# Fp32 value loads, bf16 bias factors and an earlier first FFN block in a one-core attention and maxout-FFN kernel

## The chip, the core and the metric

The kernel runs on one core of a Trainium2 chip. Its time is the device time of one execution in microseconds. Lower is better. The core's engines are named as in the profile: PE is TensorE (PEld its weight loads), ACT is ScalarE, DVE is VectorE, POOL is GpSimd and SP is SyncE. SP, ACT and POOL issue DMAs, and each does so in its own program order.

## What is computed

Attention with a relative position bias, and behind it a feed-forward layer that takes the largest of three products:

```python
batch, n_heads, seq, head_dim = (8, 8, 576, 64)          # 32 bias buckets
scores = (q @ k.T) / sqrt(64) + bias_table[bucket(|i - j|)]
attn = exp(scores - max); attn /= sum
x = (attn @ v)                                            # as [4608 tokens, 512]
h = max(x @ w1, x @ w2, x @ w3)                           # d_ff = 768
out = h @ w_out                                           # [4608, 512] float32
```

All inputs are float32 in DRAM. The bias of a head depends on |i - j| alone, and is the same for every distance beyond some 128.

## The kernel before

**The bias.** Instead of adding the bias to the scores, the kernel multiplies the exponentials by exp(bias - bias at the far end), which is 1 outside a band around the diagonal. The factors are made once: a one-hot matrix `pick` of distances by buckets and the `table` are multiplied on PE (`spread`, fp32), ACT takes the exponential with the negated far value `negc` as its bias into `w_sb` (and a mirrored half), ACT writes this row to DRAM (`w_dr`), and SP reads it back with shifted rows as `hank`, in two loads of four heads each. `times_band`, `times_band_pair` (DVE) multiply the exponentials by parts of `hank`; `bandt`, a turned copy that POOL makes in `make_bandt`, serves the left keys.

**Attention.** A batch is 8 heads in four pairs (`hp` 0 to 3). For a pair, keys and queries lie transposed in `kT` and `qT`. `scores` makes products of two key tiles with 256 queries for both heads in PSUM and one exponential of 128x1024 on ACT into `e4`. 576 is 4 x 128 + 64: the last 64 keys of both heads are handled by `left_keys`, the last 64 queries by `left_queries`, both into `el`. `attend(b, hp, e4, el, half)` makes the sums with the values (`vx`, tails in `vt`) for half 0 (256 queries) or half 1 (the other 320), and returns `quotients`, which divides on DVE into `x_sb`. `x_transposes` turn that into `xT`, FFN's input.

**Batch 0** ("batch one" of the title) has no time to prefetch, so it is written out by hand. Heads 0 to 3's first two query tiles and all keys come as fp32 by the SP and ACT queues into borrowed parts of `xT` (`q32`, `k32`), and are cast by `cast_keys`, `act_copy` and `dve_copy`; the other queries, the tails and all the values come through POOL's queue, which casts on the way (`load_main`, `load_tail`, and for `vx` one load for each head). Products on zeros (`on_zeros`, `keep_warm`) run on PE in idle stretches. The batch has two passes over the four pairs: pass one takes queries 0 to 255, pass two the rest. In pass one a step makes `visit` (two `scores`), the next pair's `first_transposes`, and left keys; the bands of pairs 0 and 1 are multiplied in its last step. The sums of a pair are put in the list `late` and popped by `next_late` in pass two: half 0 of pairs 0 and 1 in its first step, of pairs 2 and 3 in the second, then half 1 of pair 0 in the third. `behind` holds a step's band multiplies with `hank` and `bandt` (`late_bands`, `products`) for the next step.

**The queues.** `inorder` keeps an instruction in program order on its engine. On POOL the order is: batch 0's loads; `load_w(0)`; then `load_second`: keys and queries of batch 1's first pair, tails, `load_w(1)`, `make_bandt`, the other keys and queries, a spread of the first pair, batch 1's values and `load_w(2)`.

**FFN.** `add_ffn` cuts the work on a group of tokens into portions and puts them in `pending`; `fill(n)` takes portions of up to n products of a block and issues them between attention's. In a portion list f, m, g are the first, second and third gate's products of a block and o the output. For the first 256 tokens `add_ffn(0, QS)` is called in pass two's fourth step; their third gate and output are kept in `deferred` and come with the next group.

Of the kernel before, what the change touches and what calls it, by code (L numbers as in the profile page):

```python
# [39 lines left out]
def kernel(  # L40
# [12 lines left out]
    nc = tc.nc  # L53
# [180 lines left out]
    q32 = borrow(2, 2 * KT * D).rearrange("p (t h d) -> p t h d", t=2, h=KT)  # L234
# [25 lines left out]
    table = stage.tile([NB, H], F32, name="table")  # L260
    nc.gpsimd.dma_start(out=table[:], in_=bias_table)
    ident = const.tile([P, P], BF16, name="ident")
# [5 lines left out]
    nc.scalar.preload_act_table_set("natural_log_exp_and_others")  # L268
    for h in range(2):
        load_32(q, h, q32, nc.sync, 2)  # L270
    for h in range(2, H):
        load_32(k, h, k32, nc.sync)
# [6 lines left out]
    nc.gpsimd.iota(ids[:, 0:NW], pattern=[[1, NW]], base=0, channel_multiplier=0)  # L279
    nc.gpsimd.iota(ids[:, NW:], pattern=[[0, 1]], base=0, channel_multiplier=1)  # L280
    pick = xT[0:NB, 1, spare].bitcast(F32)
    zeros = xT[:, 1, NTOK - CH :]
    inorder(nc.vector.memset(zeros, 0.0))
    constants(0)
    inorder(nc.vector.memset(qtail[1][64:, :, :], 0.0))
    dve_copy(pick[:], ids[:])
    ranges = _bucket_ranges(S, NB, 128)
# [3 lines left out]
    for vv in range(single, NB):  # L291
        if ranges[vv] is not None:
            lo, hi = ranges[vv]
            assert hi <= P or vv == NB - 1
            inorder(nc.vector.memset(pick[:, lo : min(hi, NW)], float(vv)))
    inorder(nc.vector.tensor_scalar(
        out=pick[:, 0:NW], in0=pick[:, 0:NW], scalar1=pick[:, NW:], scalar2=None, op0=ALU.is_equal,
    ))
    constants(1)
    load_main(q, 0, KT, H, batch[0][0], 0, 2)  # L300
    load_tail(k, 0, 0, H, k_diag)
    load_main(q, 0, 0, H, batch[0][0], 2, KT)
    load_q_tail(0)
    load_tail(v, 0, 0, H, v_diag)
    for h in range(H):
        in_turn(0, nc.gpsimd.dma_start(out=vx[0][:, :, h, 0:D], in_=main_part(v, 0)[:, :, h, :]))
# [13 lines left out]
    on_zeros(warm[:, 0:CH], 9)  # L320

    act_copy(batch[0][0][:, 0:2, 0:2, :], q32[:, :, 0:2, :])
    w_sb = stage.tile([H, WL], BF16, name="w_sb")

    def spread_bias():
        spread = ps_a.tile([H, NW], F32, tag="a", name="spread")
        mm(spread[:], lhsT=table[:], rhs=pick[:, 0:NW])
        negc = stage.tile([H, 1], F32, name="negc")
        inorder(nc.vector.tensor_scalar(
            out=negc[:], in0=spread[:, HALF:], scalar1=-1.0, scalar2=None, op0=ALU.mult,  # L330
        ))
        for out_, in_ in ((w_sb[:, HALF:], spread[:]), (w_sb[:, 0:HALF], spread[:, HALF:0:-1])):
            inorder(nc.scalar.activation(out=out_, in_=in_, func=ACTF.Exp, bias=negc[:]))
        inorder(nc.scalar.dma_start(out=w_dr[:], in_=w_sb[:]))
# [58 lines left out]
    def ffn(t0, nt, last, tiled=False):  # L393
# [278 lines left out]
        else:  # L672
# [75 lines left out]
    def first_transposes(hp):  # L748
# [6 lines left out]
        for t in range(2):  # L755
            tr(tq[:, P * t : P * t + P], batch[0][0][:, t, hs, :].rearrange("p h d -> p (h d)"), ident[:])
        for t in range(KT):
            tr(tp[:, P * t : P * t + P], batch[0][1][:, t, hs, :].rearrange("p h d -> p (h d)"), ident[:])
        e = K if hp < 2 else L
        if e > K:  # L760
            tr(tp[:, K:L], ktail[0][:, hp, :], ident[:])
        dve_copy(qk[0][0][:, hp, 0:QS], tq[:, 0:QS])
        dve_copy(qk[0][1][:, hp, 0:e], tp[:, 0:e])
# [289 lines left out]
    cast_keys(0)  # L1053
    spread_bias()
    first_transposes(0)
    on_zeros(warm[:, 0:CH])
    for h0 in (0, KT):
# [10 lines left out]
    load_w(0)  # L1068
    batch[1] = load_tiles()
# [30 lines left out]
    for hp in range(HP):  # L1100
# [12 lines left out]
        if hp == HP - 1:  # L1113
            bands(0)
            bands(1)
        late.append(lambda hp=hp, e4=e4, el=el: attend(0, hp, e4, el, 0))
        keep_warm(1 if hp == 2 else 2)
# [3 lines left out]
        while hp and lefts:  # L1121
            lefts.pop(0)()
    load_second()
# [8 lines left out]
    for hp in range(HP):  # L1132
# [24 lines left out]
        if hp < 2:  # L1157
            quotients()
            if hp == 0:
                bands(2)  # L1160
# [9 lines left out]
            quotients = next_late()  # L1170
            quotients()
            if hp == 0:
                bands(3)
            behind.append(lambda late_bands=late_bands, hp=hp, el=el: (late_bands(), products(hp, el)))
        else:
            if behind:
                behind.pop()()
            if hp == 3:
                quotients()
                add_ffn(0, QS)  # L1180
                fill(8)
            keys()
            if hp == 2:
                quotients()
            queries()
            late_bands()
            if hp == 2:
                x_transposes(2, 0)
                x_transposes(3, 0)
            else:  # L1190
# [240 lines left out]
```

## Time and profile before

| what | value |
|---|---|
| median of 3 timed runs | 307.15 us (306.98 to 308.83) |
| span of the profiled execution, first to last instruction | 305.2 us |
| the profiled execution's own time | not stated on the page apart from its span |
| PE, DVE, ACT, POOL busy over the span | 97%, 68%, 66%, 47% |
| granted TensorE clock | 1.000 |
| DMA | 40.51 MB in 165776 packets, 154584 of them under 512 B |

A busy share is an average over stages with different limits. Batch 0 takes about the first 32 us, and what limits it is read from the rows of that stretch. A row of the timeline gives the start in us, the duration in us, the engine (with a q where only its sequencer issued a DMA), the line, the operation, output and inputs with their shapes, a count, and in brackets the idle time before it with what ended it.

### The profile page before, as it was taken

The page shows a single profiled execution, that of the slowest core. Times are in us where ns is not written, and L with a number is a line of the kernel's source. Part 1 is how long each engine was busy: PE and PEld are TensorE (multiplying, and loading weights), DVE is VectorE, ACT ScalarE, POOL GpSimd, SP SyncE. Part 2 cuts the span into 40 slices and gives each one's busy share as a digit, 9 for nine tenths or more (in the row PEclk, how much of TensorE's full clock was granted, in tenths as well). Part 3 has the DMA queues.
Part 4 walks back from the last instruction along what each step waited for, and adds up shares of the span by engine and source line. Part 5 has one row for each costly group of instructions (what it writes and reads, how often), then busy time and mean ns, then how long its engine had stood idle before and what let it go on. Part 6 is the DMA issues. An engine that isn't in the chain of part 4 may idle for free.

```text
span 305.2 us, 11001 instructions
## 1 busy us (share of the span) xinstructions
PE 295.5 (97%) x4745; PEld 183.7 (60%) x4745; DVE 206.3 (68%) x455; ACT 201.3 (66%) x270; POOL 143.7 (47%) x199
## 2 busy tenths in 40 slices
PE   8789999999999999999999999999999999999995
PEld 2367877765656676567666766676667654444442
DVE  6489888777776677676777677767776765453552
ACT  3999988977786787768776877677777720222211
POOL 8989677725839746774676469462000000000000
PEclk9999999999999999999999999999999999999999
DMA  9999999999999999999999999999623013202003
GB/s 160 187 203 194 176 137 120 114 165 128 223 150 121 150 131 205 174 143 192 181 139 135 202 162 146 138 197 171 79 46 140 6 40 94 84 0 108 31 0 137
DMA packets 165776, 40.51 MB, mean 133 GB/s; under 512 B 154584, under 2 KB 161248, under 8 KB 165728
## 3 DMA queue, kind: packets, MB, share of 16 engines
q0 software_dynamic: 105664, 16.66, 95.5%
q1 hardware_dynamic: 58304, 22.69, 41.6%
q8 instruction: 37, 0.61, 0.8%
q10 hardware_dynamic: 1760, 0.47, 0.7%
q14 instruction: 11, 0.09, 0.1%
HBM read 35.39 MB, written 9.45 MB: 147 GB/s over the span
## 4 chain that ended last, share of the span: by engine, by line
PE 80%; ACT 7%; DMA 6%; DVE 3%; SPq 2%; issue 1%; DVEq 0%; ACTq 0%
PE psp L109 32%; PE ps L109 15%; PE a L109 12%; PE sc L109 8%; PE pso L109 6%; ACT e L827 5%; DMA kT<-ktail 5%; PE sct L109 2%; PE warm L109 1%; PE scq L109 1%; ACT el L827 1%; SPq L738 1%; SPq L731 1%; DVE e L807 1%; DMA out_dram<-osb 1%
## 5 line engine op out<-in xcount | busy, mean ns | idle before, releaser
L827 ACT ACTIVATE e<-sc 128x1024 bf16<-128x1024 f32 x128 | 129.0, 1026 | 29.3 <-PE sc L109 28.0
L109 PEld LDWEIGHTS <-w_bf 64*128 64x128 bf16 (+1 forms) x1112 | 75.8, 95 | 55.3 <-issue 1.9
L109 PE MATMUL psp<-xT,w_bf 64*128 64x512 bf16 x784 | 97.2, 376 | 0.0
L807 DVE TENSOR_TENSOR e<-e,hank 128x512 bf16<-128x512 bf16 (+2 forms) x120 | 56.1, 473 | 13.9 <-ACT e L827 13.2
L109 PE MATMUL ps<-xT,w_bf 128*128 128x512 bf16 (+1 forms) x328 | 59.1, 332 | 0.0
L109 PE MATMUL sc<-qT,kT 64*128 64x256 bf16 (+1 forms) x352 | 48.5, 319 | 2.3 <-ACT e L827 1.1
L109 PEld LDWEIGHTS <-kT 64*128 64x128 bf16 (+1 forms) x712 | 30.0, 94 | 24.8 <-issue 6.8
L109 PE MATMUL a<-vx,e 64*128 64x65 bf16 (+1 forms) x1664 | 44.9, 190 | 0.0
L199 POOL DMA_DIRECT2D k_sb<-in_k_dram x48 | 36.2, 764 | 17.8 <-DMA vx<-in_v_dram 7.8
L199 POOL DMA_DIRECT2D q_sb<-in_q_dram x48 | 36.4, 767 | 15.1 <-DMA vx<-in_v_dram 5.7
L109 PEld LDWEIGHTS <-e 64*128 64x128 bf16 (+1 forms) x1664 | 40.8, 95 | 4.3
L109 PEld LDWEIGHTS <-hT 64*128 64x128 bf16 (+1 forms) x462 | 28.3, 95 | 18.7 <-DVE hT L551 1.6
L167 POOL DMA_DIRECT2D vx<-in_v_dram x28 | 24.8, 893 | 19.5 <-PE a L109 5.4
L109 PE MATMUL psp<-wo_bf,hT 64*128 64x256 bf16 (+1 forms) x360 | 31.7, 305 | 0.0
L421 ACT ACTIVATE m<-ps 128x512 bf16<-128x512 f32 x14 | 8.4, 597 | 34.3 <-PE ps L109 34.3
L827 ACT ACTIVATE el<-sct 128x576 bf16<-128x576 f32 (+2 forms) x36 | 21.7, 605 | 14.0 <-PE sct L109 13.9
L109 PEld LDWEIGHTS <-el 64*128 64x128 bf16 (+1 forms) x676 | 26.4, 94 | 7.0 <-issue 4.4
L109 PE MATMUL a<-vt,el 64*128 64x65 bf16 (+1 forms) x260 | 29.5, 198 | 0.2 <-DVE m L511 0.2
L551 DVE TENSOR_TENSOR hT<-psp,m 128x1024 bf16<-128x1024 f32 (+1 forms) x20 | 18.7, 956 | 9.1 <-PE psp L109 9.1
L109 PE MATMUL pso<-wo_bf,hT 128*128 128x512 bf16 (+2 forms) x102 | 21.7, 366 | 0.0
L430 DVE TENSOR_TENSOR m<-ps,m 128x512 bf16<-128x512 f32 x14 | 9.7, 692 | 17.0 <-PE ps L109 17.0
L537 DVE TENSOR_TENSOR m<-psp,m 128x1024 bf16<-128x1024 f32 x15 | 18.4, 1225 | 3.3 <-PE psp L109 3.1
(82 smaller groups left out, 292.8 us busy)
## 6 DMA issues: line engine op xcount, KB each, us to landing
out_dram<-osb SPq DMA_DIRECT2D x35, 256.0 KB, 4.7
vx<-in_v_dram POOLq DMA_DIRECT2D x28, 128.0 KB, 6.7
q_sb<-in_q_dram POOLq DMA_DIRECT2D x50, 64.0 KB, 5.3
k_sb<-in_k_dram POOLq DMA_DIRECT2D x48, 64.0 KB, 5.3
w_bf<-in_moe_w_dram POOLq DMA_DIRECT2D x2, 512.0 KB, 8.5
xT<-in_k_dram SPq DMA_DIRECT2D x6, 128.0 KB, 4.5
hank<-w_dr SPq DMA_DIRECT2D x2, 384.0 KB, 5.7
w_bf<-in_moe_w_dram POOLq DMA_DIRECT2D x1, 768.0 KB, 8.1
```

What stands on the lines that cost most here:

```text
L109: made = inorder(nc.tensor.matmul(*args, **kw))
L167: in_turn(b, nc.gpsimd.dma_start(out=dst[:, t, h0:h1, :], in_=x[:, t, h0:h1, :]), P * (h1 - h0))
L199: in_turn(b, nc.gpsimd.dma_start(out=dst[:, g, :, par, :], in_=part), KT * P)
L421: nc.scalar.activation(out=st[fb]["m0"][:], in_=ps0, func=ACTF.Copy)
L430: inorder(nc.vector.tensor_tensor(out=m[:], in0=ps1, in1=st[fb]["m0"][:], op=ALU.max))
L537: return lambda: inorder(nc.vector.tensor_tensor(out=m[0][:], in0=ps1(), in1=m[0][:], op=ALU.max,))
L551: inorder(nc.vector.tensor_tensor(out=out_[:, i : i + n], in0=ps2()[:, i : i + n], in1=m[0][:, i : i + n], op=ALU.max,))
L731: inorder(nc.sync.dma_start_transpose(out=made[j][:, g, 0 : KT * P].rearrange("p (t n) -> p t n", t=KT), in_=batch[b][j][:, g].rearrange(" ...
L738: inorder(nc.sync.dma_start_transpose(out=made[j][:, :, KT * P : KT * P + n], in_=(qtail, ktail)[j][b % 2][0:n].rearrange("p h c -> p (h c)"),
L807: put(nc.vector.tensor_tensor(out=e4[:, t, :, lo:hi], in0=e4[:, t, :, lo:hi], in1=hank[:, 2 * hp : 2 * hp + 2, c0:c1][:, :, ::-1], op=ALU. ...
L827: made = nc.scalar.activation(out=out_, in_=in_, func=ACTF.Exp, scale=inv_sqrt_d)
```

## The change

The bias factors: the far row of the table is loaded a second time, to all 32 partitions; DVE subtracts it, ACT takes the exponential of the 32x8 differences into bf16 `factor`, and the product with `pick`, now bf16 too, gives the factors themselves, which ACT copies. The table's loads go from POOL to ACT's queue, the two iotas go to the front of POOL's order, the keys of head 0 go to the front of SP's.

The loads of batch 0: only heads 0 and 1 of the first query tiles come as fp32; heads 2 to 7 go through POOL. The values come as fp32 by SP into `v32`, those of the first pair ahead of `hank` and the others behind it, and POOL casts them pair by pair (`cast_values`): the first pair ahead of `load_w(0)`, the other three behind it and ahead of `load_second`. Batch 1's constants are set in pass one's first step.

The order of pass one: the first transposes are parted, with the bias product between keys and queries; bands of pairs 0, 1 and 2 are multiplied in it (pair 2's right behind it), and half 0 of pair 0's sums is made in its last step. Fewer products on zeros are made. In pass two's first step come the sums of pairs 1 and 2, in the second those of pair 3 and one transposition of `x_sb` more; FFN's first 256 tokens begin in the third step instead of the fourth, so that a portion more is issued by the end of the pass. The next group's portions are put in another order, with the deferred third gates later.

```diff
     def constants(i):
-        inorder(nc.vector.memset(ktail[i][:], 0.0))
-        if i == 0:
-            inorder(nc.vector.memset(qtail[i][64:, :, :], 0.0))
+        if i:
+            inorder(nc.vector.memset(ktail[i][:], 0.0))
+        inorder(nc.vector.memset(qtail[i][64:, :, :], 0.0))
...
-    q32 = borrow(2, 2 * KT * D).rearrange("p (t h d) -> p t h d", t=2, h=KT)
+    q32 = borrow(2, 4 * D).rearrange("p (t h d) -> p t h d", t=2, h=2)
...
-    nc.gpsimd.dma_start(out=table[:], in_=bias_table)
-    make_identity(nc, ident[:])
-    load_32(k, 0, k32, nc.scalar)
+    load_32(k, 0, k32, nc.sync)
     load_32(k, 1, k32, nc.scalar)
-    for h in range(2, KT):
-        load_32(q, h, q32, nc.scalar, 2)
+    inorder(nc.scalar.dma_start(out=table[:, 0, :], in_=bias_table))
+    inorder(nc.scalar.dma_start(out=table[:, 1, :], in_=last_row))
...
-    nc.gpsimd.iota(ids[:, 0:NW], pattern=[[1, NW]], base=0, channel_multiplier=0)
-    nc.gpsimd.iota(ids[:, NW:], pattern=[[0, 1]], base=0, channel_multiplier=1)
+    inorder(nc.gpsimd.iota(ids[:, 0:NW], pattern=[[1, NW]], base=0, channel_multiplier=0))
+    inorder(nc.gpsimd.iota(ids[:, NW:], pattern=[[0, 1]], base=0, channel_multiplier=1))
+    load_main(q, 0, 2, H, batch[0][0], 0, 2)
+    make_identity(nc, ident[:])
...
-    constants(1)
-    load_main(q, 0, KT, H, batch[0][0], 0, 2)
+    constants(0)
     load_tail(k, 0, 0, H, k_diag)
+    load_tail(v, 0, 0, H, v_diag)
     load_main(q, 0, 0, H, batch[0][0], 2, KT)
     load_q_tail(0)
-    load_tail(v, 0, 0, H, v_diag)
-    for h in range(H):
-        in_turn(0, nc.gpsimd.dma_start(out=vx[0][:, :, h, 0:D], in_=main_part(v, 0)[:, :, h, :]))
+    v32 = borrow(0, KT * H * D).rearrange("p (t h d) -> p t h d", t=KT, h=H)
+
+    def cast_values(hp):
+        h = slice(2 * hp, 2 * hp + 2)
+        inorder(nc.gpsimd.tensor_copy(vx[0][:, :, h, 0:D], v32[:, :, h, :]))
...
-    on_zeros(warm[:, 0:CH], 9)
+    on_zeros(warm[:, 0:CH], 6)
+    cast_keys(0)
+    inorder(nc.vector.tensor_tensor(out=less[:], in0=table[:, 0, :], in1=table[:, 1, :], op=ALU.subtract))
+    factor = stage.tile([NB, H], BF16, name="factor")
+    inorder(nc.scalar.activation(out=factor[:], in_=less[:], func=ACTF.Exp))
...
-        mm(spread[:], lhsT=table[:], rhs=pick[:, 0:NW])
-        negc = stage.tile([H, 1], F32, name="negc")
-        inorder(nc.vector.tensor_scalar(
-            out=negc[:], in0=spread[:, HALF:], scalar1=-1.0, scalar2=None, op0=ALU.mult,
-        ))
+        mm(spread[:], lhsT=factor[:], rhs=pick)
         for out_, in_ in ((w_sb[:, HALF:], spread[:]), (w_sb[:, 0:HALF], spread[:, HALF:0:-1])):
-            inorder(nc.scalar.activation(out=out_, in_=in_, func=ACTF.Exp, bias=negc[:]))
+            act_copy(out_, in_)
...
-                portions = [x for gs, _ in deferred for x in gs]
-                for fb in range(n_fb):
-                    portions += [[f[fb], m[fb]], [g[fb]]]
+                held = [x for gs, _ in deferred for x in gs]
+                portions = [[f[0], m[0]], [f[1], m[1]]] + held[:1] + [[f[2], m[2]]] + held[1:] + [[x] for x in g]
...
+        for step in (queries, keys, put_queries, put_keys) if hp else (keys, spread_bias, queries, put_keys, put_queries):
+            step()
...
     first_transposes(0)
     on_zeros(warm[:, 0:CH])
+    cast_keys(1)
+    load_values(0, 2)                      # SP, fp32, one load for each head
     for h0 in (0, KT):
         load_hank(h0, h0 + KT)
-    dve_copy(batch[0][0][:, 0:2, 2:KT, :], q32[:, :, 2:KT, :])
-    cast_keys(1)
+    load_values(2, H)
+    cast_values(0)
...
     load_w(0)
+    for hp in range(1, HP):
+        cast_values(hp)
...
+        if hp == 0:
+            constants(1)
+        if hp >= 2:
+            bands(hp - 2)
         late.append(lambda hp=hp, e4=e4, el=el: attend(0, hp, e4, el, 0))
-        keep_warm(1 if hp == 2 else 2)
+        quotients = next_late() if hp == HP - 1 else None
+        if hp < 2:
+            keep_warm(2)
...
+        if quotients:
+            quotients()
+    bands(2)
     load_second()
...
             if hp == 0:
-                bands(2)
+                bands(3)
...
             if hp == 1:
                 x_transposes(1, 0)
+                x_transposes(2, 0)
...
-            if hp == 3:
-                quotients()
+            if hp == 2:
+                x_transposes(3, 0)
                 add_ffn(0, QS)
-                fill(8)
+            quotients()
+            fill(8)
             keys()
```

More of the change, by code (lines that the diff above doesn't have):

```diff
@@ L259 @@
     batch[0] = load_tiles()
-    table = stage.tile([NB, H], F32, name="table")
-    nc.gpsimd.dma_start(out=table[:], in_=bias_table)
-    ident = const.tile([P, P], BF16, name="ident")
-    make_identity(nc, ident[:])
-    load_32(k, 0, k32, nc.scalar)
+    ranges = _bucket_ranges(S, NB, 128)
+    far = next(i for i, r in enumerate(ranges) if r and r[0] <= HALF < r[1])
+    table = stage.tile([NB, 2, H], F32, name="table")
+    load_32(k, 0, k32, nc.sync)
     load_32(k, 1, k32, nc.scalar)
-    for h in range(2, KT):
-        load_32(q, h, q32, nc.scalar, 2)
-    nc.scalar.preload_act_table_set("natural_log_exp_and_others")
+    last_row = bass.AP(tensor=bias_table.tensor, offset=bias_table.offset + far * H, ap=[[0, NB], [1, H]])
+    inorder(nc.scalar.dma_start(out=table[:, 0, :], in_=bias_table))
+    inorder(nc.scalar.dma_start(out=table[:, 1, :], in_=last_row))
     for h in range(2):
         load_32(q, h, q32, nc.sync, 2)
+    nc.scalar.preload_act_table_set("natural_log_exp_and_others")
     for h in range(2, H):
@@ L278 @@
     ids = xT[0:NB, 0, spare].bitcast(mybir.dt.int32)
-    nc.gpsimd.iota(ids[:, 0:NW], pattern=[[1, NW]], base=0, channel_multiplier=0)
-    nc.gpsimd.iota(ids[:, NW:], pattern=[[0, 1]], base=0, channel_multiplier=1)
-    pick = xT[0:NB, 1, spare].bitcast(F32)
+    inorder(nc.gpsimd.iota(ids[:, 0:NW], pattern=[[1, NW]], base=0, channel_multiplier=0))
+    inorder(nc.gpsimd.iota(ids[:, NW:], pattern=[[0, 1]], base=0, channel_multiplier=1))
+    load_main(q, 0, 2, H, batch[0][0], 0, 2)
+    ident = const.tile([P, P], BF16, name="ident")
+    make_identity(nc, ident[:])
+    bucket = xT[0:NB, 1, spare].bitcast(F32)
+    pick = xT[0:NB, 2, 0:NW]
     zeros = xT[:, 1, NTOK - CH :]
     inorder(nc.vector.memset(zeros, 0.0))
[L284 to L287, printed above, removed]
+    inorder(nc.vector.memset(ktail[0][:], 0.0))
+    dve_copy(bucket[:], ids[:])
     single = 0
@@ L754, in first_transposes, with queries, keys, put_queries @@
         tq = tp[:, L:] if hp else ps_f.tile([P, 2 * CH], BF16, tag="ff", name="tq1")
[L755 to L758, printed above, removed]
         e = K if hp < 2 else L
[L760 to L763, printed above, removed]
+        def queries():
+            for t in range(2):
+                tr(tq[:, P * t : P * t + P], batch[0][0][:, t, hs, :].rearrange("p h d -> p (h d)"), ident[:])
+        def keys():
+            for t in range(KT):
+                tr(tp[:, P * t : P * t + P], batch[0][1][:, t, hs, :].rearrange("p h d -> p (h d)"), ident[:])
+            if e > K:
+                tr(tp[:, K:L], ktail[0][:, hp, :], ident[:])
+        def put_queries():
+            dve_copy(qk[0][0][:, hp, 0:QS], tq[:, 0:QS])
+        def put_keys():
+            dve_copy(qk[0][1][:, hp, 0:e], tp[:, 0:e])
+        for step in (queries, keys, put_queries, put_keys) if hp else (keys, spread_bias, queries, put_keys, put_queries):
+            step()
     def last_keys():
@@ L1169 @@
                 scores(*(x[:, 1, :] for x in qk[0]), begun[0][0], 1, 0)
-            quotients = next_late()
-            quotients()
-            if hp == 0:
-                bands(3)
+                quotients = next_late()
+                quotients()
             behind.append(lambda late_bands=late_bands, hp=hp, el=el: (late_bands(), products(hp, el)))
```

22 lines of the change are left out of this document (8 added, 14 removed).

## Prediction, made before the changed kernel was run

> **What bounds the kernel now.** I read the page first, then the busy time by stretches of ten microseconds, then the timeline of each engine up to 35 us, then the DMA queues by window.
>
> ```profile
> span 305.2 us, 11001 instructions
> PE 295.5 (97%) x4745; PEld 183.7 (60%) x4745; DVE 206.3 (68%) x455; ACT 201.3 (66%) x270; POOL 143.7 (47%) x199
> ...
> 0.00:10.00 10.00, 7.82 (x42) 2.77 (x42) 6.19 (x40) 4.72 (x7) 8.89 (x19) 1.00 1.24 169
> 10.00:20.00 10.00, 7.96 (x108) 4.50 (x105) 5.32 (x15) 9.54 (x15) 9.25 (x14) 1.00 1.66 191
> 20.00:30.00 10.00, 9.65 (x176) 7.22 (x173) 9.83 (x30) 9.68 (x18) 9.58 (x13) 1.00 1.41 197
> 30.00:40.00 10.00, 10.00 (x168) 8.19 (x166) 8.23 (x22) 9.20 (x17) 6.66 (x10) 1.00 1.80 181
> ```
>
> The columns of a stretch are PE, PEld, DVE, ACT, POOL, clock, DMA share and GB/s. Over the span TensorE is the bound. The change, however, edits the first 35 us, and there it is not: from 10 to 30 us ScalarE is busy 19.2 of 20 us, and GpSimd, which issues most loads, 18.8 of 20. After that nearly every microsecond is TensorE's. So whatever batch 0 gains or loses before about 32 us is carried to the end, less what later waits absorb. The span is 305.2 us and the median of the timed runs 307.15; I put the 1.95 us between them around any span.
>
> **The opening.** These rows of GpSimd, ScalarE, TensorE and VectorE set the first exponential.
>
> ```profile
> 1.29 0.66 POOL L261 DMA_DIRECT2D table<-in_bias_table_dram  x1 [0.85 <-POOLq L1415]
> ...
> 6.38 0.82 ACT L333 ACTIVATE w_sb<-spread,negc 8x256 bf16<-8x256 f32 x2 [1.75 <-DVE negc L329]
> 7.23 0.53 ACTq L334 DMA_DIRECT2D w_dr<-w_sb  x1
> 7.81 3.77 ACT L827 ACTIVATE e<-sc 128x1024 bf16<-128x1024 f32 x4 [0.61 <-PE sc L109]
> ...
> 5.14 1.02 PE L109 MATMUL spread<-xT,table 32*8 32x256 f32 x2
> 7.69 0.28 PE L113 MATMUL tp<-ident,q_sb 128*128 128x128 bf16 x2
> ...
> 2.92 0.28 DVE L126 CAST xT<-xT 32x257 f32<-32x257 int32 x1 [0.22 <-POOL xT L280]
> 4.93 0.43 DVE L126 CAST k_sb<-xT 128x512 bf16<-128x512 f32 x1
> ```
>
> Before, the bucket ids reach VectorE at 2.92 because GpSimd first issues the table's load (0.66) and begins the identity. The changed order puts both iotas first: 0.66 earlier at the least, I take 1.1 with the identity's two operations that also go behind them, so the first key cast moves from 4.93 to about 3.8. The spread is one bf16 product in place of an fp32 one of 1.02, and the scaling of negc goes; then two copies of the size of the two ScalarE pieces (0.82) and the 0.53 issue follow. I get the bias table's write at 6.1 in place of 7.23 and the first exponential at 6.65 in place of 7.81. If the broadcast row of the table lands late, the subtraction on VectorE waits with the key and query copies behind it, and the gain is 0.6; so 0.6 to 1.15, and I take 1.1. Three fewer products on zeros cost nothing, since their time held none of this.
>
> That gain is not kept. Queries of heads 2 and 3 now come through GpSimd with those of 4 to 7. In these rows the last number is the median time from issue to landing in us, ahead of it the size of one load.
>
> ```profile
> q_sb<-in_q_dram POOLq DMA_DIRECT2D x2, 64.0 KB, 4.2
> q_sb<-in_q_dram POOLq DMA_DIRECT2D x2, 128.0 KB, 4.9
> ```
>
> The two issues come right behind the iotas, which end near 1.8 by the 1.1 above, so at about 1.8 and 2.6, and land 4.2 to 4.9 later (loads of 64 and 128 KB; these are 96), the second at 6.8 to 7.5. The second pair's transposes stood at 7.69; they gain 0.2 to 0.9, I take 0.5, and with them pass one on ScalarE.
>
> **The first pair's sums in pass one.** They need the band multiplies of pair 0, hence the band's load.
>
> ```profile
> 10.81 0.92 SPq L340 DMA_DIRECT2D hank<-w_dr  x2
> ...
> DMA to landing us min/median/max: 5.0/5.7/6.4
> ...
> 15.89 0.69 DVE L822 TENSOR_TENSOR e<-e,hank 128x1024 bf16<-128x1024 bf16 x1 [0.33 <-DMA hank<-w_dr]
> 16.50 0.28 DVE L807 TENSOR_TENSOR e<-e,hank 128x256 bf16<-128x256 bf16 x1
> 16.41 0.45 ACT L827 ACTIVATE el<-sct 128x256 bf16<-128x256 f32 x1
> 19.48 0.70 PE a L109 x18
> ```
>
> With the write 1.1 earlier the band's load is issued at 9.7 and its first half lands 5.0 later, 14.7. Two multiplies (0.97) end at 15.7, and only then do the sums (0.70 for such a group) and behind them the last left keys go out on TensorE, so that ScalarE sees those at 16.6 to 16.8; before it had them at 16.41, and 0.5 sooner is where pass one would stand. The gain of pass one is used up in this wait. Pass two starts about when it did: 0, between -0.5 and +0.6 (the upper end if the late query tiles, now behind the value tails in GpSimd's queue, hold the transposes ahead of the sums). Nothing else queues behind: VectorE had idle time there (5.32 of 10 busy).
>
> **The values and GpSimd's queue.** This is the term that decides.
>
> ```profile
> 9.42 5.96 POOL L306 DMA_DIRECT2D vx<-in_v_dram  x8
> 15.30 0.82 POOL L1066 DMA_DIRECT2D w_bf<-in_moe_w_dram  x1
> 16.04 0.77 POOL L247 DMA_DIRECT2D xT<-in_k_dram  x1
> 17.53 0.71 POOL L247 DMA_DIRECT2D xT<-in_q_dram  x1 [0.72 <-DMA vx<-in_v_dram]
> 18.27 0.70 POOL L177 DMA_DIRECT2D qtail<-in_q_dram  x1
> 18.96 1.25 POOL L188 DMA_DIRECT2D ktail<-in_k_dram  x2
> 20.18 1.52 POOL L1066 DMA_DIRECT2D w_bf<-in_moe_w_dram  x2
> 21.67 1.79 POOL L356 COPY bandt<-hank 64x768 bf16<-64x768 bf16 x2
> ...
> DMA to landing us min/median/max: 3.2/5.5/6.4
> ...
> 23.92 0.25 DVE L907 TENSOR_TENSOR el<-el,bandt 128x192 bf16<-128x192 bf16 x1
> 24.25 0.22 PE L109 MATMUL a<-vt,el 128*128 128x130 bf16 x1
> ```
>
> Eight value issues (5.96) leave GpSimd. Four casts come: a bandt copy takes 0.9 for 768 elements a partition, so 0.6 by elements for 512, or 0.9 at most; I take 0.6. What matters is what they wait for. The cast of the last pair waits until the last two value loads have landed, and everything of load_second stands behind it on GpSimd: the packed keys and queries, the tails, the second weights and the copies of bandt. Before, that block needed only issue slots and ran while the values were still in flight: begun at 16.04, bandt ready at 23.46, and its first user on VectorE at 23.92, with TensorE's sums right behind at 24.25. There was 0.46 us of slack.
>
> When do the last values land? The DMA engines are full in this stretch.
>
> ```profile
> DMA packets 1945, 0.47 MB, mean 237 GB/s; under 512 B 1945, under 2 KB 1945, under 8 KB 1945
> DMA packets 3477, 0.45 MB, mean 148 GB/s; under 512 B 3469, under 2 KB 3477, under 8 KB 3477
> DMA packets 2200, 0.88 MB, mean 220 GB/s; under 512 B 1256, under 2 KB 2200, under 8 KB 2200
> ```
>
> These are 3 to 5 us (fp32 loads), 9 to 12 us (loads with a cast) and 12 to 16 us, when the band's load runs beside them. About 970 (fp32) to 1160 (cast) small packets a microsecond is what the engines do; with the band's load it is 550. Keys, queries, values and tails are the same number of packets in both kernels, and the last values are behind all of it and behind the band on SyncE's queue. So they land where they landed: the eight issues end at 15.4, the last begins 0.75 earlier at 14.6, and the median of the landing row, 5.5, makes 20.1. The bounds: the band done at 9.7 + 0.5 + 6.4 = 16.6 and six loads of 512 packets in 3 us behind it is 19.6; 18.4 if 1.2 of those 3 us overlap the band; and 23.5 with the whole first weight load ahead, which now goes out at about 12.3 (768 KB, 3.9 us at the 197 GB/s of 20 to 30 us, when such loads run). I take 20.1, the row of the same loads.
>
> Then: 20.1 + cast 0.6 + issues 4.9 (0.77 + 0.71 + 0.70 + 1.25 + 1.52, less overlaps) + bandt 1.8 = 27.4, in place of 23.46. VectorE stops at the first bandt multiply, in order, with the third pair's band multiplies and copies behind it; TensorE stops at the second half of pair 0's sums, in order, and ScalarE runs dry after the exponentials already scored. TensorE resumes at 27.65 in place of 24.25: **+3.4 us**, between +1.7 (18.4) and +6.8 (23.5). Removing the wait there would show the next late thing, the second gate's weights, issued just ahead of bandt.
>
> **What FFN's earlier start gives.** The first gate block moves from the fourth step to the third, so one block more is done when batch 1 begins.
>
> ```profile
> 33.49 1.04 PE L109 MATMUL ps<-xT,w_bf 128*128 128x256 bf16 x8
> ```
>
> Such a block takes 0.97 to the next row's start, and TensorE is full from 30 us on: **-1.0 us**; 0 if ScalarE (9.20 of 10 there) holds the pace. The new order of the portions moves no work in or out. Sum: 0 + 3.4 - 1.0 = +2.4 on 305.2, 307.6, and with 1.95 around it **309.5**.
>
> **Two rules of the skill.**
>
> ```profile
> 25.80 0.67 DVE L907 TENSOR_TENSOR el<-el,bandt 128x192 bf16<-128x192 bf16 x1
> q0 software_dynamic: 1848, 0.23, 89.5%
> q1 hardware_dynamic: 2277, 0.56, 73.0%
> ```
>
> The multiply at 25.80 lies beside GpSimd's copy and takes 0.67, not 0.25: 0.4 more beside a copy. Four more copies could cost VectorE up to 1.7, in stretches where it then waits anyway; I cost it at 0, and at up to 0.5 if that wait is short. The Trainium skill ("GPSIMD Engine Reference", section 1, Specifications) says that GpSimd's memory interface is shared with VectorE and contended by instructions with two SBUF inputs; the row agrees, and by that rule the four casts would be a charge of their own.
>
> From 5 to 9 us the two queues moved 1848 and 2277 packets, so both get turns. The Trainium skill ("DMA: Bandwidth & Descriptors", Queues, rings and completion order) says that an engine goes round the queues it has work for, a packet at a time; by that rule the large weight packets take every other turn from the last values, which is the second rival.
>
> **Rivals.** (1) *Faster:* bandt is not late. It decides where the last values land by about 16.5, so that the block of 7.3 us ends at 23.8. Then what is left is 0.5 of pass one and the 1.0 of the block: 305.7. For it: GpSimd is freed of 5.96 us and the values come without a cast. Against: the packet counts, by which nothing puts the last values ahead of 18. (2) *Slower still:* the first weights, issued three microseconds earlier, go ahead of the values: landing at 22 to 23.5, TensorE +5.3 to +6.8, so 311.4 to 312.9. (3) *The move does nothing:* pass two is late for other reasons, or ScalarE still has work during the stop, and two thirds of it are hidden: 307.3 (3.4 becomes 1.1). That FFN joins in the third step only in program order, its second gate waiting for weights that are issued behind the casts, belongs here too.
>
> **How the numbers follow.** Chances: forecast 0.45 (307.9 to 311.0), rival 1 0.25 (305.0 to 306.5), rival 2 0.15, rival 3 0.15. Range 305.5 to 311.8, which leaves out the better part of rival 1's lower half and rival 2's upper. One per cent is 3.07 us, about what a measurement of this kernel can tell from no change: above 310.2 lie rival 2 and some 0.4 of the forecast, 0.33; below 304.1 only rival 1 with no wait at all, 0.07; within, 0.60.
>
> **What would show it.** Right: GpSimd's last cast ends near 20.8, bandt near 27.5, the first bandt multiply has an idle gap of over 2 us before it ended by GpSimd, and the sums on TensorE a gap behind it; the first exponential at 6.6 to 7.2. Wrong: bandt before 24, no gap on VectorE at its first user, or the last value load landed by 17. A TensorE gap in pass one over 1 us would mean that the band, not bandt, sets the time.

## Result: 3.8% slower, and the profile after

| | before | after |
|---|---|---|
| median (lowest to highest), us | 307.34 (306.98 to 308.83), 4 runs | 319.57 (318.55 to 320.43), 4 runs |
| span of the profiled execution, us | 305.2 | 316.8 |
| ratio to before, 95% interval | | 1.0376 (1.0332 to 1.042) |

The change costs 12.2 us. The forecast was 309.5 with a range to 311.8; the time lies outside it. First the page after, the stretches of ten microseconds that the prediction showed of before, and three short stretches (columns as there: PE, PEld, DVE, ACT, POOL, clock, DMA share, GB/s).

```profile
span 316.8 us, 10992 instructions
PE 297.8 (94%) x4738; PEld 186.2 (59%) x4738; DVE 204.9 (65%) x454; ACT 201.8 (64%) x271; POOL 139.6 (44%) x194
...
0.00:10.00 10.00, 6.79 (x34) 2.71 (x36) 4.96 (x34) 4.37 (x7) 7.89 (x17) 0.92 1.25 159
10.00:20.00 10.00, 7.72 (x95) 4.43 (x91) 6.71 (x22) 8.98 (x13) 2.84 (x4) 0.91 1.42 225
20.00:30.00 10.00, 6.22 (x99) 3.79 (x95) 3.56 (x11) 6.28 (x11) 5.69 (x10) 0.83 0.78 105
30.00:40.00 10.00, 7.55 (x100) 5.65 (x101) 5.13 (x16) 4.61 (x8) 9.73 (x13) 0.83 1.43 178
...
24.00:26.00 2.00, 0.91 (x18) 0.78 (x17) 0.00 (x0) 0.00 (x0) 1.58 (x3) 0.86 0.00 0
26.00:28.00 2.00, 2.00 (x20) 0.95 (x19) 1.41 (x4) 1.72 (x5) 2.00 (x4) 0.50 0.76 94
32.00:34.00 2.00, 2.00 (x25) 1.71 (x26) 1.97 (x9) 0.38 (x1) 1.96 (x4) 0.56 1.27 204
```

The work did not grow much: ScalarE is busy 201.8 us (201.3 before) and TensorE 297.8 (295.5). From 20 to 30 us TensorE is busy 6.22 where it was 9.65, and runs 99 products where it ran 176. From 24 to 26 us VectorE, ScalarE and the DMA engines all stand still. GpSimd, once at 9.25 of 10 in the second stretch, is at 2.84: it waits. And the clock, 1.00 in all four rows of before, is 0.50 and 0.56 behind the stops.

The waits of TensorE over the first 100 us (in total, times, longest) and the timelines of GpSimd, VectorE and TensorE:

```profile
PE a L109 <- POOL vx L311: 3.2, 2, 2.9
PE a L109 <- DVE el L923: 2.8, 1, 2.8
...
PE sc L109 <- ACT kT L123: 1.1, 1, 1.1
PE ps L109 <- ACT xT L123: 0.9, 1, 0.9
...
14.56 0.61 POOL L311 CAST vx<-xT 128x512 bf16<-128x512 f32 x1 [5.86 <-DMA xT<-in_v_dram]
18.48 1.64 POOL L311 CAST vx<-xT 128x512 bf16<-128x512 f32 x2 [2.59 <-DMA xT<-in_v_dram]
24.42 0.61 POOL L311 CAST vx<-xT 128x512 bf16<-128x512 f32 x1 [4.31 <-DMA xT<-in_v_dram]
29.80 1.78 POOL L362 COPY bandt<-hank 64x768 bf16<-64x768 bf16 x2
...
31.62 0.26 DVE L923 TENSOR_TENSOR el<-el,bandt 128x192 bf16<-128x192 bf16 x1 [4.17 <-POOL bandt L362]
...
25.09 0.40 PE L109 MATMUL a<-vx,e 128*128 128x65 bf16 x8 [2.92 <-POOL vx L311]
31.94 0.23 PE L109 MATMUL a<-vt,el 128*128 128x130 bf16 x1 [2.79 <-DVE el L923]
32.99 1.92 PE L109 MATMUL ps<-xT,w_bf 128*128 128x256 bf16 x8
```

There are two stops where the prediction had one. At 25.09 the sums of pair 3 wait for the last cast itself; at 31.94 those of pair 0's second half wait, through VectorE, for `bandt`. The first FFN block then takes 1.92 us, where the same group took 1.04 before: half clock.

### The profile page after: what moved, and what is told of

It is laid out like the page before. It is cut to its first block, busy times and chain, and to the rows that moved or that the text cites. A ratio compares the mean times of both kernels' runs of the same rounds, so it can differ in the third digit from the quotient of the medians.

```text
span 316.8 us, 10992 instructions
## 1 busy us (share of the span) xinstructions
PE 297.8 (94%) x4738; PEld 186.2 (59%) x4738; DVE 204.9 (65%) x454; ACT 201.8 (64%) x271; POOL 139.6 (44%) x194
## 4 chain that ended last, share of the span: by engine, by line
PE 84%; DMA 6%; ACT 3%; SPq 2%; POOL 2%; issue 1%; DVE 0%; POOLq 0%; ACTq 0%
PE psp L109 35%; PE ps L109 18%; PE a L109 13%; PE sc L109 8%; PE pso L109 6%; PE sct L109 2%; DMA xT<-in_v_dram 2%; ACT e L843 2%; DMA w_dr<-w_sb 2%; SPq L1075 1%; DMA xT<-in_k_dram 1%; PE scq L109 1%; DMA out_dram<-osb 1%; PE tp L113 1%; POOL bandt L362 1%
## 5 line engine op out<-in xcount | busy, mean ns | idle before, releaser
L109 PEld LDWEIGHTS <-w_bf 64*128 64x128 bf16 (+1 forms) x1112 | 77.1, 95 | 56.3 <-issue 2.5
L823 DVE TENSOR_TENSOR e<-e,hank 128x512 bf16<-128x512 bf16 (+2 forms) x120 | 56.8, 478 | 15.4 <-ACT e L843 14.7
L109 PE MATMUL ps<-xT,w_bf 128*128 128x512 bf16 (+1 forms) x328 | 59.8, 336 | 0.9 <-ACT xT L123 0.9
```

The source lines that it names most:

```text
L109: made = inorder(nc.tensor.matmul(*args, **kw))
L823: put(nc.vector.tensor_tensor(out=e4[:, t, :, lo:hi], in0=e4[:, t, :, lo:hi], in1=hank[:, 2 * hp : 2 * hp + 2, c0:c1][:, :, ::-1], op=ALU. ...
```

## Experiments

The table gives the median, the ratio to before with its interval, and, read from the starts of ScalarE's exponentials in each profile, by how many us the 3rd, 9th (pass two begins), 15th and 23rd (in batch 1) of them are later than before. A lag comes from one execution, a median from several.

| run | us | ratio (95%) | 3rd | 9th | 15th | 23rd |
|---|---|---|---|---|---|---|
| after | 319.57 | 1.0376 (1.0332, 1.0420) | 0.74 | 1.21 | 9.70 | 12.28 |
| e1 values back | 311.69 | 1.0149 (1.0079, 1.0218) | 1.06 | 2.93 | 3.96 | 6.53 |
| e2 weights behind casts | 316.48 | 1.0294 (1.0217, 1.0371) | 1.52 | 2.01 | 8.83 | 11.41 |
| e3 bandt early | 314.44 | 1.0239 (1.0173, 1.0305) | 1.38 | 1.80 | 5.80 | 8.48 |
| e4 both | 313.77 | 1.0213 (1.0148, 1.0279) | 0.81 | 1.24 | 4.51 | 7.99 |
| e5 = e1, old portions | 309.71 | 1.0091 (1.0062, 1.0119) | 0.71 | 1.44 | 2.41 | 3.19 |
| e6 = e5, FFN back | 309.08 | 1.0070 (1.0035, 1.0105) | 1.53 | 1.83 | 1.49 | 1.93 |
| e7 opening alone | 308.94 | 1.0054 (1.0035, 1.0073) | 0.86 | 1.30 | 1.80 | 1.80 |
| e8 = e7, four heads | 309.24 | 1.0071 (1.0039, 1.0102) | 1.48 | 2.01 | 2.48 | 2.49 |
| e9 = e8, table first | 308.26 | 1.0039 (1.0018, 1.0060) | 0.46 | 0.51 | 1.54 | 1.55 |
| e10 values first | 320.94 | 1.0456 (1.0411, 1.0502) | 4.18 | 9.71 | 10.99 | 13.56 |
| e11 = e1, zeros in a gap | 312.16 | 1.0162 (1.0116, 1.0208) | 0.33 | 2.04 | 3.40 | 5.98 |
| e12 = e7, nine zeros | 309.56 | 1.0097 (1.0060, 1.0135) | 0.88 | 1.26 | 2.17 | 2.17 |
| e13 before, six zeros | 307.56 | 1.0028 (1.0002, 1.0054) | 0.58 | 0.19 | 1.82 | 1.82 |
| e14 = e9, nine zeros | 309.01 | 1.0079 (1.0050, 1.0109) | 0.32 | 0.93 | 1.56 | 1.55 |
| e15 factors alone | 307.95 | 1.0052 (1.0028, 1.0077) | 0.05 | 0.04 | 1.04 | 1.04 |

The kernel before, timed beside them on the same chips, had medians of 306.40 (e1 to e4), 307.10 (e5 to e11) and 307.12 (e12 to e15). What follows calls the distance to that median the time above before. None of the variants beats the kernel before.

### The values' way: e1 to e4 and e10

e1 takes the values back to GpSimd's casting loads, the rest stays changed.

```diff
-    load_values(0, 2) ... load_values(2, H); cast_values(0) ... cast_values(3)
+    for h in range(H):
+        in_turn(0, nc.gpsimd.dma_start(out=vx[0][:, :, h, 0:D], in_=main_part(v, 0)[:, :, h, :]))
```

> The changed kernel with the values of batch 0 loaded as before: eight casting loads on GpSimd behind the query tails, no fp32 values, no casts; all else stays. Theory A (the values' way sets the loss: the last casts hold sums and the whole block of load_second with bandt): both long TensorE gaps of the changed kernel (2.9 us before the third pair's sums, 2.8 us before the second half of pair 0's sums) go, the lag against the kernel before at the 15th exponential falls from 9.7 us to under 2, and the time is 306 to 309 us. Rival B (the later opening, the half clock and the new FFN order carry a good part): the time stays at 311 or above.

Measured 311.69, 5.3 above before, so the values' way is worth 6.9 of the 12.2 by these times. The rows place it: from the 9th to the 15th exponential the lag grows by 8.49 in the kernel after and by 1.03 in e1. Both stops are gone, as theory A had it, and `bandt` is done at 23.93:

```profile
21.83 2.10 POOL L359 COPY bandt<-hank 64x768 bf16<-64x768 bf16 x2
```

The 5.3 that stay are not of this cause; the time is above 311, as rival B had it. e2 moves `load_w(0)` behind the last cast; e3 moves `make_bandt` ahead of casts 1 to 3; e4 does both.

```diff
 e2: -    load_w(0)
      for hp in range(1, HP):
          cast_values(hp)
     +    load_w(0)
 e3:  load_w(0)
     +    make_bandt()          # and out of load_second
      for hp in range(1, HP):
```

> The changed kernel with the first weights' load moved behind the last cast of values, so that it takes no DMA time from them. Theory A (the first weights starve the last values): the last value load lands near 20 us instead of 24, the gap before the third pair's sums shrinks from 2.9 us to under 0.5, bandt is ready at about 28 instead of 31.5, and the time falls by 3 to 4 us to about 316. Rival C (SyncE issues the last values late behind the band, whoever else loads): they land at 23 or later all the same and the time stays within 1 us of 319.6 or gets worse, since FFN's weights come later.

> The changed kernel with the two copies of bandt ahead of the casts of pairs 1 to 3, behind the first weights' issue; the casts and load_second stay where they are. Theory A: the gap before the second half of pair 0's sums (2.8 us; 4.2 us on VectorE) goes, the one before the third pair's sums (2.9) stays, time 314 to 316.5. Rival D (behind bandt the next thing, keys or weights of load_second, is as late): the time stays above 318.

> Both moves: bandt's copies ahead of the casts of pairs 1 to 3, the first weights behind them. Theory A: both gaps go or shrink below 1 us, time about 311 to 313; what remains against the kernel before is the opening (1 us) and FFN's weights. Rival: the first weights, now issued near 20 us and landing near 28, take the place of the removed waits, and the time is no better than that of bandt's move alone.

GpSimd's rows and TensorE's waits of e2, then of e3, then of e4:

```profile
22.60 0.62 POOL L311 CAST vx<-xT 128x512 bf16<-128x512 f32 x1 [1.75 <-DMA xT<-in_v_dram]
28.71 1.77 POOL L362 COPY bandt<-hank 64x768 bf16<-64x768 bf16 x2
PE a L109 <- DVE el L923: 4.4, 1, 4.4
```

```profile
17.73 2.08 POOL L362 COPY bandt<-hank 64x768 bf16<-64x768 bf16 x2 [1.07 <-DMA hank<-w_dr]
25.11 0.62 POOL L311 CAST vx<-xT 128x512 bf16<-128x512 f32 x1 [3.67 <-DMA xT<-in_v_dram]
```

```profile
21.16 0.62 POOL L311 CAST vx<-xT 128x512 bf16<-128x512 f32 x1 [0.26 <-DMA xT<-in_v_dram]
PE ps L109 <- DMA w_bf<-in_moe_w_dram: 1.5, 1, 1.5
...
PE a L109 <- POOL vx L311: 1.0, 1, 1.0
```

In e2 the last cast comes 1.8 earlier and the stop of the sums that wait for it shrinks to 0.3, but `bandt` still stands behind all of load_second and costs a stop of 4.4. In e3 that stop is gone and the one for the casts is left, 1.8 in two parts. In e4 the stop for `bandt` is gone and 1.0 of the other is left: by the times above before 4.9 us are won of 6.9 (12.2 to 7.4), although FFN now waits 1.5 for its weights. That is only 0.7 better than e3, and the runs of the two overlap, so e4's rival is not excluded: the late weights take back most of what their move gave. So the weights ahead of the values and the copies behind them each cost their part, and even without weights in the way the last cast ends at 23.2 in e2 and at 21.8 in e4, not 20.7. Why is told by the chain (start, length) and SyncE's rows of the kernel after:

```profile
11.08 0.92 SPq L346 DMA_DIRECT2D hank<-w_dr  x2
12.04 5.37 SPq L1075 DMA_DIRECT2D xT<-in_v_dram  x6
...
6.28 4.78 DMA w_dr<-w_sb
16.91 7.39 DMA xT<-in_v_dram
```

The six loads stand in program order behind the band, which waits until 11.08 for the write of 6.28 to land. Their issues then take 5.37 us, and the last goes out at 16.91. e10 puts all eight ahead of the band.

```diff
-    load_values(0, 2)
+    load_values(0, H)
     for h0 in (0, KT): load_hank(h0, h0 + KT)
-    load_values(2, H)
```

> The changed kernel with all eight fp32 value loads ahead of the band's loads on SyncE's queue. Theory A2 (the last values are late because they stand behind the band's wait on that queue, and the weights then go ahead of them): the last value load lands by 18 us, the last cast ends by 19, bandt is ready by 26 instead of 31.5, the gap before the third pair's sums is gone; the band lands 1.5 to 3 us later and the sums of pass one wait that long; time 312 to 315. Rival A (the DMA engines are simply full, and the weights take what there is): the last cast ends after 21 and the time is above 317.

```profile
7.17 7.86 SPq L1075 DMA_DIRECT2D xT<-in_v_dram  x8
16.32 0.92 SPq L346 DMA_DIRECT2D hank<-w_dr  x2
...
11.42 0.51 ACTq L340 DMA_DIRECT2D w_dr<-w_sb  x1
...
18.15 0.62 POOL L311 CAST vx<-xT 128x512 bf16<-128x512 f32 x1 [0.23 <-DMA xT<-in_v_dram]
26.52 2.22 POOL L362 COPY bandt<-hank 64x768 bf16<-64x768 bf16 x2 [2.96 <-DMA hank<-w_dr]
...
PE a L109 <- DVE e L838: 3.7, 1, 3.7
```

The casts end at 18.77, 6.3 earlier: the order on SyncE did hold the values back. The time got worse, against the 312 to 315 expected, since the band goes out at 16.32 in place of 11.08, TensorE waits 3.7 for the band's multiplies and `bandt` has no source until 26.5. Two things hold the band. The eight issues keep SyncE until 15.03. And ScalarE issued the factors' write only at 11.42, 5.1 later than in the kernel after and behind a landing of keys by the profile; it landed at 16.31, and the first exponential, behind it on ScalarE, is 4.17 late. Why the write waited was not settled, so e10 does not tell what the order on SyncE alone would cost.

### Portions and FFN: e5 and e6

e5 is e1 with the old order of the next group's portions; e6 also starts FFN in the fourth step again.

```diff
 e5: -  held = ...; portions = [[f[0], m[0]], [f[1], m[1]]] + held[:1] + [[f[2], m[2]]] + held[1:] + [[x] for x in g]
     +  portions = [x for gs, _ in deferred for x in gs]
     +  for fb in range(n_fb):
     +      portions += [[f[fb], m[fb]], [g[fb]]]
 e6: -  add_ffn(0, QS)            # hp < 3 branch; and fill(8) in each step
     +  if hp == 3: add_ffn(0, QS); fill(8)
```

> The kernel with the values back on GpSimd (311.7 us), and the next group's portions in their old order; FFN still joins in the third step. Theory E (the new order puts a product that needs the last transposed sums of batch 0 first, so TensorE waits 0.9 us for them and VectorE's maxima come late): 310 to 311 us, the wait of FFN's products on transposed sums goes. Rival: the order is worth nothing, 311.7 within 0.5.

> As the one before, and FFN joins in the fourth step of pass two again. Theory F (with a portion less left for batch 1's first step, nothing covers the copies of the transposed keys there, and TensorE waits 1.1 us for them): the lag does not grow between the 17th and the 23rd exponential any more, 309 to 310 us. Rival (the prediction's own term): the early join is worth 1 us, so that this is 1 us slower than with the old portions alone.

e5 is 2.0 faster than e1 by the times and 2.7 by the times above before. The two ran on different chips, and their intervals overlap, but the rows place it: between the 21st and the 23rd exponential each of the seven runs with the new order (after, e1 to e4, e10, e11) loses 1.79 us, and e5 and e6 lose nothing. Some 0.3 of it comes back by the 29th. So the order costs 1.5 to 1.8 us; e1's profile was already 1.5 behind e5's at the 9th exponential, ahead of any difference between the programs. The loss is where the wait for `xT` (0.9) of the list above stands: the new list begins with first and second gates, which need the last transposes of batch 0, and leaves TensorE nothing to do while ScalarE copies them. These waits of e5 show that the one for `kT` (1.1) is another matter:

```profile
PE sc L109 <- ACT kT L123: 1.1, 1, 1.1
...
PE ps L109 <- ACT xT L123: 0.3, 1, 0.3
```

In e6 the wait for `kT` is gone too, so it belongs to the earlier join: from the 15th to the 21st exponential the lag grows by 0.78 in e5 and by 0.43 in e6. e6 is another 0.6 faster, less than their spread: the earlier join gained nothing and may have cost 0.6.

### The opening: e7 to e9 and e11 to e15

e7 is the kernel before with the new opening alone (e6 with both passes as before). e8 gives the queries of heads 2 and 3 back to ScalarE's queue as fp32. e9 also puts the table's loads first on SyncE, keys 0 and 1 on ScalarE and the bias product ahead of the first transposes, and has seven zero products at the start in place of six. e11 is e1 with three more zero products ahead of the second pair's transposes.

```diff
 e8: +    for h in range(2, KT): load_32(q, h, q32, nc.scalar, 2)
 e9: -    load_32(k, 0, k32, nc.sync)
     +    load_32(k, 0, k32, nc.scalar)
     -    inorder(nc.scalar.dma_start(out=table[:, 0, :], in_=bias_table))     # and row 1
     +    inorder(nc.sync.dma_start(out=table[:, 0, :], in_=bias_table))
     -    (keys, spread_bias, queries, ...)
     +    (spread_bias, keys, queries, ...)
 e11: +   if hp == 0: keep_warm(3)
```

> The kernel before with the new opening alone: bf16 factors, the table and iotas in their new places, queries of heads 2 to 7 through GpSimd; values, passes, bands, sums and FFN as before. Theory G (the opening gains 1 us on the first pair and loses 1.5 to 2 on the second, whose keys and queries land later): lag of 0.5 to 1.5 us at the 9th exponential, 306.5 to 308 us. Rival H (the opening is free, the sums in pass one cost the rest): within 0.4 us of the kernel before.

> As the one before, with the first query tiles of heads 2 and 3 loaded as fp32 on ScalarE's queue and cast on VectorE, as in the kernel before; what stays is the bias factors' new way. Theory G: the second pair's third exponential comes no later than in the kernel before, and 0.5 to 1 us is gained: 305.3 to 306. Rival: heads 2 and 3's keys are late all the same, behind two more loads on SyncE, and the time is that of the kernel before or up to 1 us more.

> The kernel before with the bf16 bias factors and the iotas first, the keys and queries on the queues of the kernel before (keys 0 and 1 and queries 2 and 3 on ScalarE's), the two small table loads first on SyncE's queue, and the bias product ahead of the first transposes; values, passes and FFN as before. Theory G (the second pair's later keys and queries are what the new opening loses): the lag at the third exponential is 0.3 us or less, the first exponential 0.7 to 1.1 us earlier, and the time 306.3 to 307.1, no worse than the kernel before. Rival (the bf16 way of the factors itself loses, through the wait for the table): the lag is 1 us or more here too, 308 or above.

> The kernel with the values back on GpSimd (311.7 us), with three more products on zeros in TensorE's wait ahead of the second pair's transposes. Theory K (TensorE falls to half clock from 9 us on because it stands idle there, and pass one then loses 1 to 1.5 us): the granted clock is 1.00 from 0 to 20 us, the lag at the 9th exponential is near 1.4 us instead of 2.9, and the time falls by 0.7 to 1.5 us. Rival: the clock falls all the same, or ScalarE holds the pace anyway; 311.7 within 0.5.

e7 costs 1.8, only 0.1 less than e6: the sums in pass one are free, and the opening holds the rest. e8 gains nothing; there VectorE waits 1.44, until 8.38, for the queries of heads 2 and 3. e9 takes back 0.7, and the first exponential then stands where it stood before (0.02 earlier), so the 0.7 to 1.1 expected there did not come. e11 gains nothing; its third exponential is 0.73 earlier than e1's, but its clock fell a little later all the same: 1.00 and 0.73 in the first two stretches of ten microseconds, 0.87 and 0.67 in e1.

ScalarE and VectorE in the opening of the kernel after, and last the same cast of before:

```profile
6.84 1.94 ACT L843 ACTIVATE e<-sc 128x1024 bf16<-128x1024 f32 x2 [0.68 <-PE sc L109]
10.37 1.94 ACT L843 ACTIVATE e<-sc 128x1024 bf16<-128x1024 f32 x2 [1.60 <-PE sc L109]
...
4.77 0.15 DVE L328 TENSOR_TENSOR less<-table 32x8 f32<-32x8 f32 x1 [0.54 <-DMA table<-in_bias_table_dram]
7.82 0.45 DVE L126 CAST k_sb<-xT 128x512 bf16<-128x512 f32 x1 [1.67 <-DMA xT<-in_k_dram]
...
7.42 0.41 DVE L126 CAST k_sb<-xT 128x512 bf16<-128x512 f32 x1
```

The first exponential is 0.97 earlier, then ScalarE waits 1.60: VectorE waits until 7.82 for the keys of heads 2 and 3, which it cast at 7.42 before without a wait. But with six zero products e7 also ran its first scores at half rate (1.03 us for eight, 0.61 before), and the kernel after its second eight (0.61, then 1.03), so I tested the zeros as the cause: nine of them in e7 (e12), six in the kernel before (e13), nine and two more in e9 (e14). e15 has the one part with a gain of its own, the bf16 factors, alone.

```diff
 e12: -    on_zeros(warm[:, 0:CH], 6)
      +    on_zeros(warm[:, 0:CH], 9)
 e13: the reverse, in the kernel before
 e14: e9 with 9 for 7, and  + if hp == 0: keep_warm(2)
 e15: the kernel before with less, factor, the bf16 product and two copies; far row on ScalarE's queue
```

> The kernel before with the new opening alone, but with nine products on zeros at the start in place of six. In the opening alone the first eight score products took 1.03 us on TensorE and the next eight 1.04, where the kernel before had 0.61 for the first. Theory K (the three products taken out let TensorE fall to half rate in the opening): 0.61 again, the third exponential no later than before, and 307.3 us, that is the 1.8 us of the opening gone. Theory L (the opening is late because the keys and queries of heads 2 and 3 land late): no gain, 309; or 309.5, if the transposes now wait 0.6 us for the zeros to end.

> The kernel before with six products on zeros at the start in place of nine, nothing else. Theory K: the first scores take 1.03 in place of 0.61, and the time rises by 1 to 2 us to 308.1 to 309. Theory L, and the prediction's own step (fewer zero products cost nothing): 307.1, no change.

> The run with the table's loads first, with nine products on zeros instead of seven and two more in the wait ahead of the second pair's transposes. Theory K: the last 1.2 us go, 307 or, with the earlier spread, 306.5. Theory L: 308.3 as without them.

> The kernel before with the bf16 factors alone: a second load of the table on ScalarE's queue, the difference, the exponential to bf16, one bf16 product in place of the fp32 one, two copies; the nine zeros, all other loads and the passes as before; batch 1's constants go behind the first key cast on VectorE. If the fp32 product was on the path of the first exponential: that comes 0.5 us earlier, at 7.3, the band's write too, and the time is 306.6. Theory K adds that TensorE keeps its rate, since nothing is taken from its zeros. Against it: the second table load puts the queries and the table of functions 0.5 us later on ScalarE, and the factors then come no earlier: 307.1, no change. The opening runs so far gained nothing by the earlier write: the band's load was issued at 11.1 with it and at 10.8 without.

The theory of the zeros falls. e12's TensorE is at full rate, and the keys are late all the same:

```profile
6.38 0.61 PE L109 MATMUL sc<-qT,kT 64*128 64x256 bf16 x8 [0.17 <-DVE qT L126]
...
8.42 0.49 DVE L126 CAST k_sb<-xT 128x512 bf16<-128x512 f32 x1 [2.09 <-DMA xT<-in_k_dram]
```

Its third exponential is 0.88 late, as in e7, and its time no better. e14's first scores run at 0.61 too, and it gains nothing on e9. e13 runs its first scores at 1.04 and is 0.4 us slower; its pass two begins 0.19 late. What it and e15 lose comes later, at another place: rows of e13, then of before, from GpSimd, VectorE and TensorE.

```profile
21.32 2.14 POOL L356 COPY bandt<-hank 64x768 bf16<-64x768 bf16 x2
22.70 0.91 DVE L807 TENSOR_TENSOR e<-e,hank 128x256 bf16<-128x256 bf16 x1
23.53 0.31 DVE L126 COPY qT<-tp 128x320 bf16<-128x320 bf16 x1
23.89 0.27 PE L113 MATMUL xp<-ident,x_sb 128*128 128x128 bf16 x2 [1.61 <-DVE qT L126]
```

```profile
21.50 0.28 DVE L807 TENSOR_TENSOR e<-e,hank 128x256 bf16<-128x256 bf16 x1
21.71 0.31 DVE L126 COPY qT<-tp 128x320 bf16<-128x320 bf16 x1
22.68 1.32 DVE L822 TENSOR_TENSOR e<-e,hank 128x1024 bf16<-128x1024 bf16 x1
```

While GpSimd copies `bandt`, VectorE's multiply takes 0.91 in place of 0.28. In the run of before the slow multiply came behind the copy of `qT`, so TensorE did not wait. In e13 VectorE is some tenths later against GpSimd, the slow multiplies come ahead of the copy, and TensorE waits 1.61. e12 has the same wait at 0.9, e9 and e15 at 1.0, e14 at 0.6, e7 at 0.5. So the opening's 1.8 is made, by e7's rows, of 1.3 by the start of pass two (the second pair's keys and queries) and 0.5 of this collision, which a few tenths turn on or off. Part of a collision is made up later: e13's lag is 1.82 at the 23rd exponential and 0.80 at the last. The gains of e15 never came: `less` waits 1.29 for the table, and the band was issued at 11.51, 0.7 later than before, though its write went out 0.46 earlier, at 6.77.

## Why the prediction was wrong

The direction and the place were right, by the mechanism of its main term; the size was off by 10 us, in five steps.

1. **"The values and GpSimd's queue" (+3.4): right chain, landing mis-sized.** "They land where they landed" failed. The last load was issued at 16.91, not 14.6, and took 7.39 to land, not 5.5; the last cast ends at 25.03 against 20.7, `bandt` at 31.58 against 27.4, TensorE resumes at 31.94 in place of 24.25: +7.7. The rest of the chain held: from the last cast's end to `bandt` it took 6.55 us, 6.7 by the working. So nearly all of the 4.3 that the term missed is the landing, 24.30 in place of 20.1. The working gave the packets to the engines without asking when SyncE could issue them, and its bound of 19.6 built on a band issued at 9.7; it was 11.08. Rival 2, the weights ahead of the values, was true on top (e2: 1.8 on the last cast). The prediction's upper bound of 23.5 for the landing was passed too: 24.30.
2. **A wait was left out.** The last cast feeds pair 3's sums before `bandt` matters. They stopped TensorE 2.92 us at 25.09. It had come to them at 22.17, so with the casts done at the forecast 20.7 it would not have stopped: this follows from step 1. It does not add to the 7.7 either, which `bandt` sets.
3. **The clock was left out.** The rows at half clock behind both stops (0.50 and 0.56) turned a block of 1.04 into one of 1.92. The Trainium skill ("TensorE: Matmul & The Clock Gate", Part 1) says that the array falls to half rate after an idle window of about 3.4 us and comes back after a busy one of about 3.4. The way back agrees: by rows of one microsecond the kernel after is at half clock from 8.4 to 11.8, 25.4 to 28.8 and 32.2 to 35.7, some 3.4 each time (an estimate from the mean clock of the first and the last row). The way down does not: the two stops are shorter than that figure, and between its first product and 8.4 no wait of TensorE was over 0.78. So what makes the clock fall here is open. What this share was of the 6.9 no run separates.
4. **"FFN's earlier start" (-1.0) and "moves no work in or out" (0) failed.** The join gained nothing (e6 faster by 0.6 without it) and the order cost 1.5 to 1.8 by the rows, 2.0 to 2.7 by the times (e5): an order moves no work, but it decides what stands ready beside a copy.
5. **The opening.** First exponential 6.84 where 6.65 was forecast: right, with some luck, since the same opening gave 6.91 to 7.59 in e1 to e7. "They gain 0.2 to 0.9" for the second pair failed: the third exponential is 0.74 late, since heads 2 and 3 have keys too, which now stand behind one load more on SyncE. "With the write 1.1 earlier the band's load is issued at 9.7" failed: the write was issued 0.95 earlier and took 4.78 us to land. So pass two, put at 0 with a bound of +0.6, began 1.21 late. The sums in pass one cost nothing, as forecast (e6 against e7: 0.1).

By the times above before: values 6.9, portions 2.7, join 0.6, pass one 0.1, opening 1.8; before rounding that is 12.2. Each is the difference of two neighbours in the row after, e1, e5, e6, e7, before, so the sum comes out by construction and confirms nothing; undone in another order the parts could differ. The differences across chips carry an error of a microsecond or so.

On contention, costed at 0 to 0.5: beside the four casts one multiply of VectorE took 0.70 in place of 0.28 (at 18.94), and no wait of TensorE followed from it; the old copies beside VectorE's multiplies did harm (0.91 for 0.28), as the rule of the Trainium skill that was quoted there ("GPSIMD Engine Reference", section 1, Specifications) would have it. On turns between queues the rows of 16 to 18 and of 18 to 20 us (packets, MB, share) say this, with the row of 18 to 20 us of e2, where the weights go out later, as the last:

```profile
q1 hardware_dynamic: 1651, 0.43, 121.6%
...
q0 software_dynamic: 253, 0.39, 107.2%
q1 hardware_dynamic: 143, 0.03, 10.9%
...
q1 hardware_dynamic: 1545, 0.38, 115.1%
```

In the second stretch, where the weights (q0) run, the values' queue (q1) moved 143 packets, a twelfth of the two microseconds before; in e2, without weights, it moved 1545. So the weights did take the engines from the values, as rival 2 had it. The rule quoted there from the Trainium skill ("DMA: Bandwidth & Descriptors", Queues, rings and completion order) lets an engine drain a whole packet, typically some 9 to 17 descriptors, before it goes on to the next queue. A packet of these rows is some 260 B (0.43 MB in 1651), and they do not tell how such packets are grouped, so the counts do not test that rule.

## What to carry to other kernels

When loads move from one engine's queue to another's, work out when each is issued there, behind which waits, before counting packets: here six loads stood behind a wait for a small write, and one slow landing held all of the engine that cast them. Whatever stands behind such a cast in program order has to be listed with its users, and the half clock that followed both stops here has to be charged too. An order of portions is a schedule of covers: keep ready work beside each copy that the next product needs.

## What the runs showed of the hardware

- A write of 8 KB to DRAM landed 4.78 us after its issue, beside the loads of the opening, and issuing it 0.95 us earlier did not let its reader start earlier (11.08 against 10.81).
- Beside the casting load of weights (253 packets, 0.39 MB) the small packets of the values came to 143 in two microseconds; without it, in e2, to 1545 in the same two.
- e1 and e5 are the same program up to batch 1. In one profile the clock from 10 to 20 us was 0.67, in the other 1.00, and the first began pass two 1.5 us later.
- With six zero products at the start TensorE's first scores took 1.03 to 1.04 in place of 0.61 in e3 to e7 and e13, though the granted clock of these stretches reads 1.00; in the kernel after and in e1, e2, e8, e10 and e11, also with six, they took 0.61. In e13, which changes nothing else, the time is 0.4 longer.
- In the kernel after the half clock came in stretches of some 3.4 us, one of them behind no wait over 0.78.
- The copy of `bandt` (64x768, twice) beside multiplies on VectorE made one of 0.28 take 0.91, and its phase against them moved the start of a step by up to 1.6 us.
